# Attention of the second sequence: float32 in chunks of 64 steps in place of pairs of float16 parts

## The chip, the cores and the metric

One core of one Trainium2 chip runs the whole program. The metric is the device time of one launch in microseconds (us), lower is better, as the median of repeated runs. Engines: TensorE (PE, its weight loads shown apart as PEld), VectorE (DVE), ScalarE (ACT), GpSimd (POOL), and SyncE (SP), which here issues nearly all DMAs.

## What is computed

Four sequences of 768 steps with 8 heads of 48 pass through a decaying linear attention, and its output goes through two gated feed-forward layers; the second normalises its input first.

```python
# attention, per sequence and head (D = 48)
for t in range(S):
    cur = outer(u * k[t], v[t])
    y[t] = r[t] @ (state + cur)
    state = w[:, None] * state + outer(k[t], v[t])
# layer 1:  x = (silu(x @ Wg) * (x @ Wv)) @ Wo            (384 -> 1536 -> 384)
# layer 2:  the same on x / rms(x) * rms_g, with its own weights
```

Attention data are float32, the weights are doubles, read as pairs of 32-bit words and decoded on the chip.

## The kernel before, in words

The feed-forward layers run in blocks of 384 tokens, eight per layer (half a sequence each). Every float32 product is made of float16 products: each operand is held as a high and a low part, and three matmuls (high·high, high·low, low·high) take the place of one. A block is 12 steps; a step is the gate product `pg`, the value product `pv` (line 820) and the output product `po` (line 830), 27 matmuls of 384 columns. Between them ACT makes the silu (934), DVE the product `sl` (942, 944), ACT its high part (948) and POOL its low part (952). Blocks run in the order (layer 1, 0), (1, 1), (1, 2), (2, 0), (1, 3), (2, 1), ...

The weights are decoded by ACT and DVE, layer 1 as 12 large pieces, layer 2 as 36 of a third of that size (lines 769 to 810). Both layers stay on the core afterwards.

Attention comes in 32 units: 4 sequences, 2 halves of 384 steps, 4 pairs of heads. A unit has four matmul stages: `a` (keys by receptances inside a chunk, to PSUM `pa`), `d` (what each chunk adds to the state, `pd`), the state recurrence on DVE (`st`, line 654), and `y` (values by the masked `a`, and the state by receptances, `py`). The first sequence (units 0 to 7, class `Unit`) does this in float32 in chunks of 128 steps. The other 24 units (`SplitUnit`) do it in chunks of 64 steps in float16 pairs: four operands, the keys `k`, the receptances `r`, the weighted keys `e` and the masked product `a`, are split by ACT (line 566) and by POOL or DVE (line 569); the values are split and put into their columns of a zeroed tile `vb` by ACT and DVE (600, 602), the states into `sb` (665, 667). Each chunk of `a` and `d` is then three float16 matmuls for each head (line 622), each chunk of `y` six of 64 columns (line 611). ACT also sums the squares of `k`, `r` and `v` (line 607) for a range check at the end.

The order of every engine's instructions is fixed when the program is built. A planner (`Plan`, lines 71 to 135) gets each job with its engine, an assumed cost and the jobs it must follow, simulates the engines and always takes the ready job with the longest chain behind it. SP's DMA issues are ordered in the same way, as "D" jobs, and stand in one queue. A unit's jobs are named `lk`, `lr`, `nk`, `nr`, `nv` (loads), `tk`, `tr`, `kg`, `rg` (transposes and weighting), `k0` to `a1` (splits), `v0`, `v1`, `s0`, `s1` (values, states), `d`, `a`, `y`, `below`, `st`, `xh`, `xl` (lines 1103 to 1142).

Of the kernel before, what the change touches and what calls it, by code (L numbers as in the profile page):

```python
# [7 lines left out]
F32 = mybir.dt.float32  # L8
# [62 lines left out]
class Plan:  # L71
# [67 lines left out]
def fast_path(ctx, tc, r, k, v, w, u, wg1, wv1, wo1, wg2, wv2, wo2, rms_g, out):  # L139
# [11 lines left out]
    NG = TB // P  # L151
    NV = 4
    N2 = TB // C2
    NU1 = 2 * HP

    const = ctx.enter_context(tc.tile_pool(name="const", bufs=1))
    wp = ctx.enter_context(tc.tile_pool(name="wp", bufs=1))
# [38 lines left out]
    wsum = c_tile([P, 2 * NW], "wsum")  # L196
    mlo = c_tile([P, 1], "mlo")

    sqs = c_tile([P, 3 * (NBLK * HP - NU1)], "sqs")

# [130 lines left out]
    class Unit:  # L331
# [195 lines left out]
    class SplitUnit(Unit):  # L527


        def stage(self, slot):  # L530
            pass

        def load(self, which):
            t = b_tile([P, NP2 * D], "rts" if which else "kts", bufs=2)
# [43 lines left out]
            nc.vector.tensor_reduce(out=self.gd, in_=self.rk, axis=AX.X, op=ALU.add)  # L578

        def diagonals(self):  # L580
            self.af = b_tile([P, N2, C2], "af")
            nc.gpsimd.tensor_mul(self.af, late["id2"].unsqueeze(1).to_broadcast([P, N2, C2]),
                                 self.gd.unsqueeze(2).to_broadcast([P, N2, C2]))

        def decayed(self):
            self.ef = b_tile([P, N2, 64], "ef")
            kv = self.nk
            nc.gpsimd.tensor_mul(
                self.ef.rearrange("p c (i n) -> p c i n", i=2),
                bass.AP(kv.tensor, kv.offset, [list(kv.ap[0]), [D, N2], [16, 2], [1, 32]]),  # L590
                late["D2"][:, self.hp].rearrange("p (i n) -> p i n", i=2).unsqueeze(1).to_broadcast([P, N2, 2, 32]),
            )
# [10 lines left out]

        def squares(self, i):
            jk = ev.tile([P, N2, D], BF16, tag="sq", name="jk")
            col = 3 * (self.n - NU1) + i
            nc.scalar.activation(out=jk, in_=(self.nk, self.nr, self.nv)[i], func=AF.Square, accum_out=sqs[:, col : col + 1])

        def passes(self, out, pairs):
# [67 lines left out]

        yscale = 2.0 ** (X1S - 3 * AB)

    units = [(SplitUnit if b else Unit)(b, half, hp, (b * 2 + half) * HP + hp)  # L680
             for b in range(B) for half in range(2) for hp in range(HP)]

    bctx = ExitStack()
# [1 line left out]
    def open_split():  # L685
        actx.close()
        late["bp"] = bctx.enter_context(tc.tile_pool(name="bp", bufs=1))
        late["stg"] = bctx.enter_context(tc.tile_pool(name="stg2", bufs=1))
        for name in ("vb", "sb"):
            late[name] = b_tile([P, 2, N2, P], name, F16)  # L690
        late["G2"], late["F2"] = b_tile([P, HP, 2 * C2], "G2"), b_tile([P, HP, C2], "F2")
        late["D2"], late["u2"] = b_tile([P, HP, 64], "D2"), b_tile([P, HP, D], "u2")
        late["id2"], late["m2"] = b_tile([P, C2], "id2"), b_tile([P, C2], "m2", I32)
        late["carry"] = [b_tile([P, D], f"carry2{hp}") for hp in range(HP)]
        for j in range(2):
            nc.sync.dma_start(out=late["u2"][64 * j : 64 * j + 64], in_=bass.AP(u.tensor, D * j, [[0, 64], [2 * D, HP], [1, D]]))

    def split_zeros(name):
        nc.gpsimd.memset(late[name], 0.0)

    def split_tables():

# [256 lines left out]
    def check_range():  # L959


        n = 2 * NBLK * NG
        ns = 3 * (NBLK * HP - NU1)
        ok = ev.tile([P, n + n // 2 + 3 * NW + ns + 1], F32, tag="sq", name="ok")
        g2 = ev.tile([P, KT], F32, tag="g2", name="g2")
        gs = ev.tile([P, 1], F32, tag="gs", name="gs")
        nc.vector.tensor_mul(g2, rmsg, rmsg)
        nc.vector.tensor_reduce(out=gs, in_=g2, axis=AX.X, op=ALU.add)
        at = 0
        for i, bound, op in ((ssall, 3.0e38, ALU.is_le), (ssall[:, : n // 2], TOK_LO * DM, ALU.is_ge),  # L970
                             (wsum[:, :NW], SUM_HI, ALU.is_le), (wsum[:, :NF], MAG_MEAN * 3 * DM, ALU.is_ge),
                             (wsum[:, NF:NW], MAG_MEAN * DM, ALU.is_ge), (wsum[:, NW:], 0.0, ALU.is_le),
                             (sqs, MS_LO * N2 * D, ALU.is_ge), (gs, GAIN_LO, ALU.is_ge)):
            m = i.shape[1]
            nc.vector.tensor_scalar(out=ok[:, at : at + m], in0=i, scalar1=bound, scalar2=None, op0=op)
# [42 lines left out]
    def last(what, J):  # L1018
        return [(what, at_step[J] + NF - 1)] if J in at_step else []
# [30 lines left out]
    for un in units[:NU1]:  # L1050
# [23 lines left out]
        else:  # L1074
# [19 lines left out]
        add(("xl", n), "V", 0.47 * m, [("xh", n)], lambda un=un, j=j: un.x_lo(x_tile(j)),  # L1094
            soon=due(j, i))
    add("split", "D", 1.25, [("xl", n) for n in range(NU1)] + [("lo", 0, f) for f in range(NF)], open_split)
    for name in ("vb", "sb"):
        add(("z", name), "G", 1.32, ["split"], lambda name=name: split_zeros(name))
    add("tables2", "V", 2.2, ["split"], split_tables)
    add("dec2", "T", 0.5, ["tables2"], split_decay)  # L1100
    add("decay2", "A", 0.6, ["dec2"], split_decay2)
    add("u2", "G", 0.8, ["split"], split_bonus)
    for un in units[NU1:]:
# [8 lines left out]
        job_("lr", "D", 1.8, [("lk", n)] + p("tr", 2), lambda un=un: un.load(1))  # L1112
        for w_, users in (("k", ("rk", "ex", "sq")), ("r", ("rk", "sq")), ("v", ("v1", "sq"))):
            job_("n" + w_, "D", 0.9, [("lk", n)] + [x for us in users for x in p(us, 2)], lambda un=un, w_=w_: un.load_natural(w_))
        job_("tk", "V", 0.85, [("lk", n)] + p("k1"), lambda un=un: un.turn("k"))
# [9 lines left out]
        job_("eg", "G", 0.8, [("sums", n), "tables2"] + p("a1"), lambda un=un: un.diagonals())  # L1125
        job_("ex", "G", 1.0, [("nk", n), "decay2"] + p("e1"), lambda un=un: un.decayed())
        job_("e0", "A", 0.42, [("ex", n)] + p("d"), lambda un=un: un.split("e", 0))
        job_("e1", "G", 0.88, [("e0", n)], lambda un=un: un.split("e", 1, nc.gpsimd))
        job_("v0", "A", 0.8, [("nv", n), ("z", "vb")] + p("y"), lambda un=un: un.values(0))
# [7 lines left out]
        job_("st", "V", 1.5, [("d", n)] + p("s1") + ([("st", n - HP)] if un.half else p("st")), lambda un=un: un.states())  # L1137
        job_("s0", "A", 0.85, [("st", n), ("z", "sb")] + p("y"), lambda un=un: un.states2(0))
# [4 lines left out]
    add("attended", "D", 0.0, [("xl", n) for n in range(NU)] + [("sq", n) for n in range(NU1, NU)], close_attention)  # L1143


    def w_jobs(q, scale, wcost, ready, ahead):
# [252 lines left out]
```

## Time and profile before

| what | value |
|---|---|
| median of 3 runs | 1048.23 us (1045.59 to 1048.25) |
| the profiled execution: its own time | 1051.98 us |
| its span | 1050.3 us |
| PE busy | 978.8 us (93%) |
| PE weight load | 604.7 us (58%) |
| DVE busy | 609.4 us (58%) |
| ACT busy | 518.7 us (49%) |
| POOL busy | 456.9 us (43%) |
| mean granted PE clock | 0.968 |

Busy shares are averages over the whole span and hide that the engines' loads change along it. The page gives the span in 40 slices of 26 us with the busy tenths of each engine, and a view of chosen stretches gives the exact microseconds. The span ends with PE's work; the profiled execution's own time is 1.7 us longer than its span.

### The profile page before, as it was taken

What the parts mean: (1) busy time and instruction counts of PE and PEld (TensorE: products, weight loads), DVE (VectorE), ACT (ScalarE), POOL (GpSimd) and SP (SyncE); (2) the same over time, 40 slices, a digit from 0 to 9 for tenths busy, and PEclk for the clock granted to TensorE, in tenths of its full rate; (3) what the DMA queues carried; (4) which work ended last, traced back from release to release, by engine and by line L of the source; (5) the groups of instructions that cost most, each with busy time, mean ns of one, the idle gap of its engine ahead of it and who ended that gap; (6) DMA issues with size and microseconds to landing.
All of it is one profiled execution on the core that took longest, in us unless ns stands there. A gap on an engine that the chain in (4) does not pass through costs nothing.

```text
span 1050.3 us, 20693 instructions
## 1 busy us (share of the span) xinstructions
PE 978.8 (93%) x8061; PEld 604.7 (58%) x8062; DVE 609.4 (58%) x1120; ACT 518.7 (49%) x1217; POOL 456.9 (43%) x502
## 2 busy tenths in 40 slices
PE   7778798897889999999999999999999999999995
PEld 4645554554555566656666666666666666666663
DVE  6999999999888754546354744645352412231111
ACT  1965566767685743536344643455343523242322
POOL 6257376545455444553355444553444223332221
PEclk8898899998999999999999999999999999999998
DMA  7997155449655421213113321222010100200000
GB/s 181 222 224 190 27 132 150 113 74 183 142 161 70 103 71 27 49 40 92 40 41 63 80 53 37 30 61 69 7 18 8 54 1 1 53 23 1 23 1 27
DMA packets 152699, 77.13 MB, mean 73 GB/s; under 512 B 115472, under 2 KB 141200, under 8 KB 152592
## 3 DMA queue, kind: packets, MB, share of 16 engines
q1 hardware_dynamic: 152208, 75.13, 31.6%
q8 instruction: 65, 1.06, 0.5%
q0 software_dynamic: 384, 0.59, 0.3%
q14 instruction: 42, 0.34, 0.1%
HBM read 66.23 MB, written 9.45 MB: 72 GB/s over the span
## 4 chain that ended last, share of the span: by engine, by line
PE 65%; DVE 13%; DMA 11%; SPq 5%; issue 3%; ACT 2%; POOL 1%; DVEq 0%; ACTq 0%; POOLq 0%
PE pg L820 20%; PE pv L820 20%; PE po L830 20%; DMA raw<-in_moe_w_out_dram 5%; DMA raw<-in_moe_w_gate_dram 3%; DVE fi L787 2%; PE py L611 2%; DVE w L810 2%; SPq L364 2%; DVE fi L789 1%; DMA xs_d<-tt 1%; DVE fi L785 1%; PE pa L622 1%; PE pd L622 1%; DVE st L654 1%
## 5 line engine op out<-in xcount | busy, mean ns | idle before, releaser
L820 PEld LDWEIGHTS <-w 128*128 128x128 f16 x3456 | 337.8, 99 | 246.8 <-issue 35.6
L952 POOL TENSOR_TENSOR hl<-sl,hh 128x384 f16<-128x384 f32 x192 | 186.3, 971 | 432.8 <-ACT hh L948 402.4
L830 PE MATMUL po<-w,hh 128*128 128x384 f16 x1152 | 281.7, 327 | 0.5 <-DVE xo L844 0.5
L948 ACT ACTIVATE hh<-sl 128x384 f16<-128x384 f32 x192 | 100.0, 521 | 342.3 <-DVE sl L942 193.9
L830 PE MATMUL po<-w,hl 128*128 128x384 f16 x576 | 187.9, 326 | 7.2 <-POOL hl L952 7.2
L820 PE MATMUL pg<-xh,w 128*128 128x384 f16 x576 | 164.2, 341 | 15.1 <-DVE sl L944 14.6
L820 PE MATMUL pv<-x2v,w 128*128 128x384 f16 x864 | 157.6, 328 | 2.5 <-ACT sl L934 2.5
L942 DVE SCALAR_TENSOR_TENSOR sl<-sl,pv 128x384 f32<-128x384 f32 x96 | 52.9, 551 | 183.6 <-PE pv L820 175.0
L820 PE MATMUL pv<-xh,w 128*128 128x384 f16 x576 | 158.2, 330 | 0.0
L820 PE MATMUL pg<-x2g,w 128*128 128x384 f16 x864 | 156.1, 326 | 2.1 <-DVE sl L942 1.7
L830 PEld LDWEIGHTS <-hh 128*128 128x128 f16 x1152 | 111.8, 98 | 74.0 <-issue 1.5
L944 DVE TENSOR_TENSOR sl<-sl,pv 128x384 f32<-128x384 f32 x96 | 52.4, 547 | 102.3 <-PE pv L820 102.1
L934 ACT ACTIVATE sl<-pg 128x384 f32<-128x384 f32 x192 | 92.8, 484 | 32.7 <-PE pg L820 30.4
L820 PE MATMUL pg<-xl,w 128*128 128x384 f16 x288 | 98.4, 342 | 0.0
L820 PE MATMUL pv<-xl,w 128*128 128x384 f16 x288 | 95.1, 330 | 0.0
L830 PEld LDWEIGHTS <-hl 128*128 128x128 f16 x576 | 56.4, 98 | 47.8 <-POOL hl L952 11.0
L787 DVE SCALAR_TENSOR_TENSOR fi<-raw,fi 128x384 int32<-128x384 int32 (+1 forms) x48 | 43.6, 915 | 1.1
L810 DVE SCALAR_TENSOR_TENSOR w<-fi,w 128x384 f16<-128x384 f32 (+1 forms) x48 | 42.6, 902 | 0.8 <-ACT w L806 0.6
L654 DVE SCALAR_TENSOR_TENSOR st<-st,p,pd 128x48 f32<-128x48 f32 x120 | 31.8, 265 | 19.3 <-PE pd L622 15.1
L789 DVE SCALAR_TENSOR_TENSOR fi<-raw,fi 128x384 int32<-128x384 int32 (+1 forms) x48 | 40.0, 848 | 0.7
L569 POOL TENSOR_TENSOR ap<-af,ap 128x384 f16<-128x384 f32 x24 | 25.1, 1044 | 33.9 <-ACT ap L566 33.9
L551 DVE STREAM_TRANSPOSE kf<-kts 128x384 f32<-128x384 f32 x24 | 20.8, 865 | 32.4 <-POOL kp L569 32.3
(190 smaller groups left out, 1257.0 us busy)
## 6 DMA issues: line engine op xcount, KB each, us to landing
raw<-in_moe_w_out_dram SPq DMA_DIRECT2D x24, 384.0 KB, 4.4
kts<-in_k_dram SPq DMA_DIRECT2D x112, 70.0 KB, 2.5
rts<-in_r_dram SPq DMA_DIRECT2D x112, 70.0 KB, 2.1
raw<-in_moe_w_gate_dram SPq DMA_DIRECT2D x12, 384.0 KB, 3.9
raw<-in_moe_w_val_dram SPq DMA_DIRECT2D x12, 384.0 KB
xs_d<-tt SPq DMA_DIRECT2D x32, 144.0 KB, 2.9
xt<-xs_d SPq DMA_DIRECT2D x32, 144.0 KB, 3.0
out_dram<-xo SPq DMA_DIRECT2D x7, 576.0 KB, 3.1
```

The costliest lines, as they stand in the source:

```text
L569: eng.tensor_sub(t[:, 1], x, t[:, 0])
L654: nc.vector.scalar_tensor_tensor(out=st[:, c + 1], in0=st[:, c], scalar=self.w64(), in1=self.pd[:, c], op0=ALU.mult, op1=ALU.add)
L787: vec.scalar_tensor_tensor(out=fis[q], in0=high, scalar=-0x40000000, in1=fis[q], op0=ALU.bitwise_and, op1=ALU.bitwise_or)
L789: vec.scalar_tensor_tensor(out=fis[q], in0=low, scalar=29, in1=fis[q], op0=ALU.logical_shift_right, op1=ALU.bitwise_or)
L810: nc.vector.scalar_tensor_tensor(out=lo, in0=fis.pop(q).bitcast(F32), scalar=2.0**WS, in1=hi, op0=ALU.mult, op1=ALU.subtract)
L820: nc.tensor.matmul(pt, a[:, kt, :], x[:, kt, :], start=i == 0, stop=i == last)
L830: nc.tensor.matmul(po[g], a[:, sl], x, start=f == 0 and i == 0, stop=f == NF - 1 and i == 2)
L934: nc.scalar.activation(out=sl, in_=job[t]["g"], func=AF.Silu, scale=2.0 ** -(WS + (X2S if J[0] else X1S)))
L942: nc.vector.scalar_tensor_tensor(out=sl, in0=sl, scalar=2.0 ** (H2S - WS - V2S), in1=job[t]["v"], op0=ALU.mult, op1=ALU.mult)
L944: nc.vector.tensor_mul(sl, sl, job[t]["v"])
L948: nc.scalar.activation(out=job[t]["h"][0], in_=job[t]["sl"], func=AF.Copy)
L952: nc.gpsimd.tensor_sub(hl, job[t]["sl"], hh)
```

## The change

Units 8 to 15 (the second sequence) become a third class, `FullUnit`: float32 like the first sequence, but with the chunks of 64 steps and the loads of `SplitUnit`. It has no splits, no copies of the values, no low part of the states and no sums of squares. The values are loaded by DMA straight into their columns of a zeroed float32 tile: even units use the bytes of `vb`, odd units two half tiles with the tag `nv`. The even units' `kf`, `af` and `ef` use the tags of `SplitUnit`, the odd units' the bytes that later hold the float16 pairs. Units 16 to 31 stay as they were; their first units wait for the last `FullUnit` in some places, and `vb` and `sb` are zeroed again after it.

```diff
-    NU1 = 2 * HP
+    NU1, NU2 = 2 * HP, 4 * HP
+    class FullUnit(SplitUnit):
+        def slot(self, which):
+            return (which + "f", which + "p")[self.par]
+        def load_v(self):
+            for j in range(2):
+                for c, m, t in late["vf"][self.par]:
+                    nc.sync.dma_start(
+                        out=t[64 * j : 64 * j + 64, :, D * j : D * j + D],
+                        in_=bass.AP(v.tensor, self.off(j) + c * C2 * D, [[D, C2], [C2 * D, m], [1, D]]))
...
+        def mm_a(self):
+            self.pa = ps.tile([P, TB], F32, tag=self.bank(1), name="pa")
+            for c in range(N2):
+                for j in range(2):
+                    q = slice(64 * j, 64 * j + 64)
+                    nc.tensor.matmul(self.pa[q, C2 * c : C2 * c + C2], self.kf[q, c], self.rf[q, c], start=True, stop=True)
+        def mm_d(self):
...
+                    nc.tensor.matmul(self.pd[q, c], self.ef[q, c], self.values_of(c)[q, D * j : D * j + D], start=True, stop=True)
+        def states2(self):
+            c = 1 - self.half
+            for j in range(2):
+                q = slice(64 * j, 64 * j + 64)
+                nc.scalar.activation(out=late["sf"][q, c:, D * j : D * j + D], in_=self.st[q, c:N2], func=AF.Copy,
+                                     scale=self.w64()[q])
+        def mm_y(self):
...
+                mms = [(self.values_of(c), self.af[:, c])]
+                if self.half or c:
+                    mms.append((late["sf"][:, c], self.rf[:, c]))
+                self.passes(self.py[0 : 2 * D, C2 * c : C2 * c + C2], mms)
+    units = [(Unit, FullUnit, SplitUnit, SplitUnit)[b](b, half, hp, (b * 2 + half) * HP + hp)
+    for name in ("vb", "nv", "sb"):
+        add(("z", name), "G", 1.32, ["split"], lambda name=name: split_zeros(name))
     for name in ("vb", "sb"):
-        add(("z", name), "G", 1.32, ["split"], lambda name=name: split_zeros(name))
+        add(("z2", name), "G", 1.32, [("y", NU2 - 1)], lambda name=name: split_zeros(name))
+    for un in units[NU1:NU2]:
...
+        job_("nv", "D", 0.9, [("lk", n), ("z", ("vb", "nv")[un.par])] + p("y", 2), lambda un=un: un.load_v())
+        job_("tk", "V", 0.85, [("lk", n)] + p("a", 2), lambda un=un: un.turn("k"))
+        job_("kg", "V", 0.55, [("tk", n), "tables2"], lambda un=un: un.weigh("k"))
+        job_("tr", "V", 0.85, [("lr", n)] + p("y", 2), lambda un=un: un.turn("r"))
+        job_("rk", "G", 1.9, [("nk", n), ("nr", n), "u2"] + p("sums"), lambda un=un: un.products())
+        job_("eg", "G", 0.92, [("sums", n), "tables2"] + p("y", 2), lambda un=un: un.diagonals())
+        job_("ex", "G", 1.06, [("nk", n), "decay2"] + p("d", 2), lambda un=un: un.decayed())
+        job_("d", "T", 0.8, [("ex", n), ("nv", n), "decay2"] + p("below") + p("y"), lambda un=un: un.mm_d())
+        job_("a", "T", 0.9, [("kg", n), ("rg", n), ("d", n)] + p("xl"), lambda un=un: un.mm_a())
+        job_("below", "V", 0.55, [("a", n), ("eg", n)], lambda un=un: un.below())
+        job_("st", "V", 1.7, [("d", n)] + p("s0") + ([("st", n - HP)] if un.half else p("st")), lambda un=un: un.states())
+        job_("s0", "A", 0.9, [("st", n), ("z", "sb")] + p("y"), lambda un=un: un.states2())
+        job_("y", "T", 2.0, [("below", n), ("s0", n), ("a", n)], lambda un=un: un.mm_y())
...
+    for un in units[NU2:]:
...
+            job_("n" + w_, "D", 0.9, [("lk", n)] + [x for us in users for x in p(us, 2)] + ([("y", NU2 - 1)] if w_ == "v" and n < NU2 + 2 else []),
+        job_("tk", "V", 0.85, [("lk", n)] + p("k1") + q_("a"), lambda un=un: un.turn("k"))
+        job_("v0", "A", 0.8, [("nv", n), ("z2", "vb")] + p("y"), lambda un=un: un.values(0))
```

## Rows read from the trace of the kernel before

**Rows 1.** The page: busy time, and tenths in 40 slices of the span.
```profile
PE 978.8 (93%) x8061; PEld 604.7 (58%) x8062; DVE 609.4 (58%) x1120; ACT 518.7 (49%) x1217; POOL 456.9 (43%) x502
PE   7778798897889999999999999999999999999995
...
DVE  6999999999888754546354744645352412231111
...
PEclk8898899998999999999999999999999999999998
```

**Rows 2.** Stretches: length, busy PE PEld DVE ACT POOL, clock, DMA share, GB/s.
```profile
125.00:350.00 225.00, 194.51 (x1790) 117.45 (x1788) 209.56 (x390) 156.06 (x419) 119.39 (x128) 0.95 0.59 128
...
350.00:1050.00 700.00, 687.28 (x5657) 422.14 (x5654) 288.71 (x561) 290.44 (x668) 267.73 (x301) 0.99 0.17 38
...
275.00:300.00 25.00, 21.38 (x208) 12.89 (x207) 21.41 (x43) 19.65 (x54) 10.31 (x11) 0.93 0.61 165
...
325.00:350.00 25.00, 25.00 (x242) 15.58 (x241) 19.34 (x41) 14.65 (x41) 10.28 (x10) 1.00 0.67 95
```

**Rows 3.** PE's waits from 125 to 350 us: us in total, times, longest.
```profile
PE pg L820 <- DVE sl L944: 7.6, 5, 3.2
PE py L611 <- DVE sb L667: 7.5, 4, 4.1
PE py L611 <- POOL ap L569: 4.7, 5, 1.4
PE pv L820 <- ACT sl L934: 2.5, 1, 2.5
PE po L830 <- POOL hl L952: 2.4, 3, 1.5
PE py L611 <- ACT ap L566: 2.3, 2, 1.3
```

**Rows 4.** Groups of instructions by shape, 125 to 350 us: busy us, mean ns.
```profile
L787 DVE SCALAR_TENSOR_TENSOR fi<-raw,fi 128x384 int32<-128x384 int32 x36 | 24.1, 676 | 1.0
...
L569 DVE TENSOR_TENSOR rp<-rf,rp 128x384 f16<-128x384 f32 x9 | 10.6, 1180 | 0.7 <-ACT rp L566 0.7
...
L602 DVE SCALAR_TENSOR_TENSOR vb<-nv,vb 64x288 f16<-64x288 f32 x16 | 10.5, 654 | 0.2
...
L569 POOL TENSOR_TENSOR kp<-kf,kp 128x384 f16<-128x384 f32 x8 | 9.0, 1119 | 2.5 <-ACT kp L566 2.5
...
L667 DVE SCALAR_TENSOR_TENSOR sb<-st,p,sb 64x240 f16<-64x240 f32 x8 | 6.9, 856 | 0.1
...
L667 DVE SCALAR_TENSOR_TENSOR sb<-st,p,sb 64x288 f16<-64x288 f32 x6 | 3.8, 636 | 0.0
```

**Rows 5.** PE's timeline, float16 units: start, us, instructions.
```profile
165.05 0.75 PE L622 MATMUL pa<-rp,kp 64*64 64x64 f16 x36
...
202.24 0.75 PE L622 MATMUL pd<-vb,ep 64*64 64x48 f16 x36
```

**Rows 6.** Line 611 alone (float16 y), a stretch with one unit.
```profile
325.00:350.00 25.00, 1.21 (x36) 1.19 (x36) 1.00 0.67 95
```

**Rows 7.** PE's timeline, float32 units of the first sequence.
```profile
26.79 0.56 PE L470 MATMUL po<-vb,kg 128*64 128x48 f32 x12 [0.25 <-ACT kg L444]
...
29.49 0.73 PE L440 MATMUL in<-uw,kr 128*128 128x2 f32 x6
...
96.29 1.23 PE L463 MATMUL att<-rt,kt 64*128 64x128 f32 x12 [0.25 <-DVE kt L391]
```

**Rows 8.** Line 507 alone (float32 y, chunks of 128), a stretch with one unit.
```profile
75.00:100.00 25.00, 2.20 (x18) 2.26 (x18) 0.93 0.76 185
```

**Rows 9.** SP's timeline: issuing the values of one unit.
```profile
200.15 1.27 SPq L546 DMA_DIRECT2D nv<-in_v_dram  x2
```

**Rows 10.** DMA issues from 125 to 350 us: count, size, median us to landing.
```profile
nv<-in_v_dram SPq DMA_DIRECT2D x20, 72.0 KB, 2.7
```

**Rows 11.** Line 787 from 125 to 350 us: duration ns min/median/max.
```profile
L787 DVE SCALAR_TENSOR_TENSOR fi<-raw,fi x36: 527/559/1297, 145.4 to 345.6; 128x384 int32<-128x384 int32 x36
```

More of the change, by code (lines that the diff above doesn't have):

```diff
@@ L197, in fast_path @@
     mlo = c_tile([P, 1], "mlo")
-    sqs = c_tile([P, 3 * (NBLK * HP - NU1)], "sqs")
+    sqs = c_tile([P, 3 * (NBLK * HP - NU2)], "sqs")
     wu_raw = a_tile([2 * HP, 4, 32], "wu_raw")
@@ L527, in fast_path @@
     class SplitUnit(Unit):
-        def stage(self, slot):
-            pass
+        def slot(self, which):
+            return which + "f"
         def load(self, which):
@@ L580, in diagonals @@
         def diagonals(self):
-            self.af = b_tile([P, N2, C2], "af")
+            self.af = b_tile([P, N2, C2], self.slot("a"))
             nc.gpsimd.tensor_mul(self.af, late["id2"].unsqueeze(1).to_broadcast([P, N2, C2]),
@@ L585, in decayed @@
         def decayed(self):
-            self.ef = b_tile([P, N2, 64], "ef")
+            self.ef = b_tile([P, N2, 64], self.slot("e"))
             kv = self.nk
@@ L605, in squares @@
             jk = ev.tile([P, N2, D], BF16, tag="sq", name="jk")
-            col = 3 * (self.n - NU1) + i
+            col = 3 * (self.n - NU2) + i
             nc.scalar.activation(out=jk, in_=(self.nk, self.nr, self.nv)[i], func=AF.Square, accum_out=sqs[:, col : col + 1])
@@ L678, in fast_path, with slot, values_of, turn @@
         yscale = 2.0 ** (X1S - 3 * AB)
-    units = [(SplitUnit if b else Unit)(b, half, hp, (b * 2 + half) * HP + hp)
+    class FullUnit(SplitUnit):
+        def slot(self, which):
+            return (which + "f", which + "p")[self.par]
[5 more added lines that the diff above has]
+                        in_=bass.AP(v.tensor, self.off(j) + c * C2 * D, [[D, C2], [C2 * D, m], [1, D]]))
+        def values_of(self, c):
+            return next(t[:, c - c0] for c0, m, t in late["vf"][self.par] if c0 <= c < c0 + m)
+        def turn(self, which):
+            tag = "rp" if which == "r" else self.slot("k")
+            t = b_tile([P, N2, C2], tag, bufs=2 if which == "r" else 1)
+            setattr(self, which + "f", t)
+            nc.vector.transpose(
+                out=t.rearrange("q c t -> q (c t)").rearrange("q (p i) -> q i p", i=NP2),
+                in_=(self.kts if which == "k" else self.rts).rearrange("q (i d) -> q i d", d=D)[:, :, 0:32],
+            )
+        def mm_a(self):
[5 more added lines that the diff above has]
+        def mm_d(self):
+            self.nd = N2 - self.half
+            self.pd = ps.tile([P, N2, D], F32, tag=self.bank(0), name="pd")
+            for c in range(self.nd):
+                for j in range(2):
[3 more added lines that the diff above has]
+            c = 1 - self.half
+            for j in range(2):
+                q = slice(64 * j, 64 * j + 64)
+                nc.scalar.activation(out=late["sf"][q, c:, D * j : D * j + D], in_=self.st[q, c:N2], func=AF.Copy,
+                                     scale=self.w64()[q])
+        def mm_y(self):
+            self.py = ps.tile([P, TB], F32, tag=self.bank(2), name="py")
+            for c in range(N2):
+                mms = [(self.values_of(c), self.af[:, c])]
+                if self.half or c:
+                    mms.append((late["sf"][:, c], self.rf[:, c]))
+                self.passes(self.py[0 : 2 * D, C2 * c : C2 * c + C2], mms)
+        yscale = 2.0 ** (X1S - 2 * AB)
@@ L690, in open_split @@
             late[name] = b_tile([P, 2, N2, P], name, F16)
+        vf, late["sf"] = (late[name].bitcast(F32).rearrange("p a c m -> p (a c m)")[:, 0 : N2 * 2 * D].rearrange(
+            "p (c m) -> p c m", m=2 * D) for name in ("vb", "sb"))
+        late["vf"] = [[(0, N2, vf)], [(i * N2 // 2, N2 // 2, b_tile([P, N2 // 2, 2 * D], "nv", bufs=2)) for i in range(2)]]
         late["G2"], late["F2"] = b_tile([P, HP, 2 * C2], "G2"), b_tile([P, HP, C2], "F2")
@@ L698, in split_zeros @@
     def split_zeros(name):
-        nc.gpsimd.memset(late[name], 0.0)
+        for t in [t for _, _, t in late["vf"][1]] if name == "nv" else [late[name]]:
+            nc.gpsimd.memset(t, 0.0)
     def split_tables():
@@ L962, in check_range @@
         n = 2 * NBLK * NG
-        ns = 3 * (NBLK * HP - NU1)
+        ns = 3 * (NBLK * HP - NU2)
         ok = ev.tile([P, n + n // 2 + 3 * NW + ns + 1], F32, tag="sq", name="ok")
@@ L1102, in fast_path @@
     add("u2", "G", 0.8, ["split"], split_bonus)
-    for un in units[NU1:]:
+    for un in units[NU1:NU2]:
         n, hp, j, i = un.n, un.hp, un.n // HP, un.n % HP
@@ L1112, in fast_path @@
         job_("lr", "D", 1.8, [("lk", n)] + p("tr", 2), lambda un=un: un.load(1))
+        for w_, users in (("k", ("rk", "ex")), ("r", ("rk",))):
+            job_("n" + w_, "D", 0.9, [("lk", n)] + [x for us in users for x in p(us, 2)], lambda un=un, w_=w_: un.load_natural(w_))
+        job_("nv", "D", 0.9, [("lk", n), ("z", ("vb", "nv")[un.par])] + p("y", 2), lambda un=un: un.load_v())
+        job_("tk", "V", 0.85, [("lk", n)] + p("a", 2), lambda un=un: un.turn("k"))
+        job_("kg", "V", 0.55, [("tk", n), "tables2"], lambda un=un: un.weigh("k"))
@@ new lines, in fast_path, with job_ @@
+        job_("y", "T", 2.0, [("below", n), ("s0", n), ("a", n)], lambda un=un: un.mm_y())
+        job_("xh", "A", 0.47 * m, [("y", n)] + last("gv", (0, j - 2)), lambda un=un, j=j: un.x_hi(x_tile(j)))
+        job_("xl", "V", 0.55 * m, [("xh", n)], lambda un=un, j=j: un.x_lo(x_tile(j)), soon=due(j, i))
+    for un in units[NU2:]:
+        n, hp, j, i = un.n, un.hp, un.n // HP, un.n % HP
+        p = lambda what, back=1: [(what, n - back)] if (what, n - back) in plan.jobs else []
+        q_ = lambda what: [(what, n - 2)] if n == NU2 else []
+        m = len(un.rows())
+        def job_(name, eng, cost, after, fn, **kw):
+            add((name, n), eng, cost, after, fn, **kw)
+        job_("lk", "D", 1.8, ["split"] + p("tk", 2) + p("lr"), lambda un=un: un.load(0))
+        job_("lr", "D", 1.8, [("lk", n)] + p("tr", 2), lambda un=un: un.load(1))
@@ L1113, in fast_path @@
         for w_, users in (("k", ("rk", "ex", "sq")), ("r", ("rk", "sq")), ("v", ("v1", "sq"))):
-            job_("n" + w_, "D", 0.9, [("lk", n)] + [x for us in users for x in p(us, 2)], lambda un=un, w_=w_: un.load_natural(w_))
-        job_("tk", "V", 0.85, [("lk", n)] + p("k1"), lambda un=un: un.turn("k"))
+            job_("n" + w_, "D", 0.9, [("lk", n)] + [x for us in users for x in p(us, 2)] + ([("y", NU2 - 1)] if w_ == "v" and n < NU2 + 2 else []),
+                 lambda un=un, w_=w_: un.load_natural(w_))
@@ L1124, in fast_path @@
         job_("sums", "V", 0.37, [("rk", n)] + p("eg"), lambda un=un: un.sums())
-        job_("eg", "G", 0.8, [("sums", n), "tables2"] + p("a1"), lambda un=un: un.diagonals())
-        job_("ex", "G", 1.0, [("nk", n), "decay2"] + p("e1"), lambda un=un: un.decayed())
+        job_("eg", "G", 0.92, [("sums", n), "tables2"] + p("a1") + q_("y"), lambda un=un: un.diagonals())
+        job_("ex", "G", 1.06, [("nk", n), "decay2"] + p("e1") + q_("d"), lambda un=un: un.decayed())
         job_("e0", "A", 0.42, [("ex", n)] + p("d"), lambda un=un: un.split("e", 0))
         job_("e1", "G", 0.88, [("e0", n)], lambda un=un: un.split("e", 1, nc.gpsimd))
-        job_("v0", "A", 0.8, [("nv", n), ("z", "vb")] + p("y"), lambda un=un: un.values(0))
+        job_("v0", "A", 0.8, [("nv", n), ("z2", "vb")] + p("y"), lambda un=un: un.values(0))
         job_("v1", "V", 0.8, [("v0", n)], lambda un=un: un.values(1))
@@ L1136, in fast_path @@
         job_("a1", "G", 0.88, [("a0", n)], lambda un=un: un.split("a", 1, nc.gpsimd))
-        job_("st", "V", 1.5, [("d", n)] + p("s1") + ([("st", n - HP)] if un.half else p("st")), lambda un=un: un.states())
-        job_("s0", "A", 0.85, [("st", n), ("z", "sb")] + p("y"), lambda un=un: un.states2(0))
+        job_("st", "V", 1.5, [("d", n)] + p("s1" if n > NU2 else "s0") + ([("st", n - HP)] if un.half else p("st")), lambda un=un: un.states())
+        job_("s0", "A", 0.85, [("st", n), ("z2", "sb")] + p("y"), lambda un=un: un.states2(0))
         job_("s1", "V", 0.8, [("s0", n)], lambda un=un: un.states2(1))
@@ L1142, in fast_path @@
         job_("xl", "V", 0.47 * m, [("xh", n)], lambda un=un, j=j: un.x_lo(x_tile(j)), soon=due(j, i))
-    add("attended", "D", 0.0, [("xl", n) for n in range(NU)] + [("sq", n) for n in range(NU1, NU)], close_attention)
+    add("attended", "D", 0.0, [("xl", n) for n in range(NU)] + [("sq", n) for n in range(NU2, NU)], close_attention)
     def w_jobs(q, scale, wcost, ready, ahead):
```

2 lines of the change are left out of this document (added).

## The prediction, made before the changed kernel was run

> **What bounds the kernel now.** I read the page's slices first. PE stays at nine tenths or more only from the thirteenth slice on; before that it is mostly at seven or eight, and there DVE is at nine and eight, and hardly anywhere later [rows 1]. So there are two regimes. After 350 us PE is the bound: busy 687 of 700 us, DVE 41% [rows 2]. From 125 to 350 us, where the layer-2 weights are decoded, DVE is busy 209.6 of 225 us (93%) while PE is busy 194.5 (86%) and idle 30.5 [rows 2]. The second sequence's attention lies in this stretch: its values are split by line 602, 16 times, two for each of its eight units, all inside it [rows 4]. Since PE carries on without a gap afterwards, the time is PE's work plus PE's idle time, and an edit here counts by what it does to both.
>
> What PE waits for, from the view of waits: 27.0 of the 30.5 us stand in six rows [rows 3]. The `y` products wait 7.5 us for the low part of the states (DVE, 667), 4.7 for the low part of the masked product (POOL, 569) and 2.3 for its high part (ACT, 566): 14.5 us, each time for a link of the splitting that the change removes. The other 12.5 us are the feed-forward steps waiting for DVE's `sl`, ACT's silu and POOL's `hl`, which are late because they stand in queues behind other work. The granted clock is 0.95 in the mean there, so some 0.05 x 225 = 11 us of full-speed time are lost too; it is 0.93 in a stretch where PE idles 3.6 of 25 us and 1.00 where it idles for none [rows 2].
>
> **The change, part by part.**
>
> *DVE loses work.* `r1` goes: 10.6 us in nine, so 9.4 for eight units. `v1` goes: 10.5 us. `s1` goes: 6.9 + 3.8 = 10.7 us for the seven units that have it inside the stretch [rows 4]. Sum 30.6 us, and DVE's load falls from 209.6 to 179 us.
>
> *POOL and ACT lose work.* POOL loses three splits of a unit, each near the 9.0 us of `kp` in eight [rows 4], about 27 of its 119 us [rows 2]. ACT loses four splits, the values' copies and the squares. Neither is near full now; what this buys is shorter queues before `hl` and the silu, and I put that into the idle time below, not into a term of its own. Added on POOL are four memsets: two more before unit 8, beside the tables and the first loads, and two behind the `y` of unit 15, for which unit 16 waits. Unit 16 feeds block (1, 4), the seventh in order, whereas at 350 us the fourth, (2, 0), is being worked on; PE has other work, and DVE then has room. I cost them at nothing; without that cover it is a few us, once.
>
> *PE gets other matmuls.* A float16 unit costs 0.75 (`d`) + 0.75 (`a`) [rows 5] + 1.21 (`y`) [rows 6] = 2.7 us. In float32 each matmul becomes two instructions in the trace: `a` for one unit of the first sequence is 12 of 128 columns and 1.23 us, `d` is 12 of 48 columns and 0.56 [rows 7], `y` is 18 of 128 columns and 2.20 [rows 8]. With chunks of 64:
> - `a`: 24 of 64 columns, the same column count, at most 1.23 us. The two heads alternate between different rows and columns of the array. 36 such float16 matmuls take 0.75 us in `a`, but 36 of the same 64 columns take 1.21 in `y` [rows 5, 6], a ratio of 0.62, so the alternation pays: 0.76 at that ratio, half (0.62) at best. I take 0.85.
> - `d`: 24 of 48 columns, at most 2 x 0.56 = 1.12, at the ratio 0.69, at best 0.56. I take 0.75.
> - `y`: 24 of 64 columns, each with a fresh weight load of 96 float32 columns. By columns alone 2.20 / 18 / 2 x 24 = 1.47 us. But six loads of 128 float32 columns with hardly a matmul behind them took 0.73 us [rows 7], 0.12 each, so 0.09 for 96 columns, which 64 columns don't cover: 24 x 0.09 = 2.2. I take 2.1, nearer to the loads.
>
> Sum 3.7, that is +1.0 us a unit and **+8 us** in all; the ends are 2.65 (nothing added) and 4.55 (+15 us). This is wholly on the path.
>
> *The chain of a unit gets shorter.* `y` follows `below` and `s0` at once. The 14.5 us of waits of `y` lose their releasers. Late next are the high part of the states on ACT and `below` on DVE, both already done when PE resumed in those waits; but DVE's queue still lies before them, so I leave 3 us. The remaining 16 us (12.5 named, 3.5 in small pieces) hang on queues that get shorter, DVE's by 15% and POOL's by 23%; I leave 12. So 15 of 30.5 us stay and **15.5 us** come back. Another way to the same number: idle by DVE's share. At 86% (21.41 of 25 us) PE idled 3.6 us, at 77% for none [rows 2]; 179 us in some 215 is 83%, between them 2.4 us in 25, or 20 us left and 10 back. I take the first, as the waits that go are named one by one, and keep the second for the range.
>
> *Clock.* Of the 11 us I take **3** back, as the gaps shrink; the ends are none and 6.
>
> *Loads.* Odd units load their values with four DMAs instead of two: two issues took 1.27 us [rows 9], so 5 us more on SP over four units, in a queue that is not full. The new wait is that the values go straight into the tile that the `y` two units earlier reads, so their load stands in SP's queue until then, with the next unit's loads and a weight piece behind it. The `a` of unit 9 is at 165 us and the `d` of unit 11 at 202 [rows 5]; landing takes 2.7 us [rows 10]. With `y` of unit 9 some ten us behind its `a`, over 20 us are left. Nothing.
>
> **Sum.** +8 - 15.5 - 3 = -10.5 us. The profiled execution took 1051.98 us (1.7 more than its span), so 1041.5; that execution is 3.75 above the median of the runs, 1048.23, and from there it is **1038 us**.
>
> **A rule weighed.** The mean of line 787 is 676 ns, its least 527 [rows 11], so DVE's operations in this stretch are stretched by something: 36 x 0.15 = 5.4 us for this line. The Trainium skill ("SBUF — State Buffer", Who interferes with whom) says that a DVE instruction with two SBUF inputs and a GpSimd instruction that reads SBUF exclude each other. By that rule the 23% less POOL work would give DVE back another 1.2 us on this line and, as an estimate, 5 us on all lines like it, of which some 3 would reach the time: 1035 instead of 1038. The spread of the row fits it but does not name POOL as the cause.
>
> **The rivals.**
> 1. *DVE was the whole bound.* All its 30.6 us count: PE's idle time falls to 5 us and 6 us of clock return. 8 - 25.5 - 6 = -23.5: 1025 us. For it: DVE at 93%. Against: PE alone would need 194.5 + 8 - 6 = 196.5 us of a stretch then 201.5 long, 97.5%, with DVE at 89%, while it idled 14% at DVE's 86% [rows 2]. Chance 0.15.
> 2. *It cancels.* The idle time by DVE's share is right (10 back) and the clock gives nothing: +8 - 10 = -2, 1046 us. Chance 0.17.
> 3. *Slower: the waits are handed on.* PE's order is fixed, and with the shorter chain the planner puts each `y` earlier, so that PE meets DVE's queue before `st` and `below` instead of the splits behind them. Only 5 us come back, while float32 costs between my value and the upper end, 11.4: +6.4, 1054.6 us. It decides from the point where less than PE's added work comes back. For it: the two longest waits in the first two rows are for DVE [rows 3]. Against: 7.0 us of the `y` waits were for POOL and ACT. Chance 0.13.
>
> My forecast has 0.55. Its own range is 1033 to 1044. The range to hold 8 in 10 takes rivals 1 and 2 in and reaches into 3: 1026 to 1050. A measurement can tell about 0.3% (3.1 us) from no change: faster 0.70 (forecast, rival 1), same 0.17 (rival 2), slower 0.13 (rival 3).
>
> **What would show it.** From 125 us to PE's saturation: PE's share at or above 91% and DVE's at or below 87%; `y` (24 instructions) near 2.1 us, `a` 0.85, `d` 0.75; no more than 3 us of waits of `y`; saturation some ten us earlier than 325. It is wrong if `y` still waits over 8 us (rival 3), if DVE stays above 90% with PE idle for 20 us or more (rival 2), or if float32 costs over 4.2 us a unit.

## The result: 1% faster

The changed kernel takes 1038.75 us (median of 6 runs, 1035.55 to 1042.67) against 1048.51 (6 runs of the kernel before, beside it); the ratio is 0.9902, 95% interval 0.9877 to 0.9928. The prediction was 1038. Measured once more, beside the last experiments, the ratio was 0.9908 (0.9883 to 0.9933). The profiled execution took 1040.54 us, its span is 1038.5.

The page after: the busy line, and PE, DVE and PE's clock in 40 slices, which answer to [rows 1].

```profile
PE 982.7 (95%) x7786; PEld 613.8 (59%) x7786; DVE 573.1 (55%) x1080; ACT 486.6 (47%) x1121; POOL 442.5 (43%) x482
...
PE   6787898989999999999999999999999999999996
...
DVE  6899997988787544655354645555342412241111
...
PEclk7889899999999999999999999999999999999998
```

The span is 11.8 us shorter, while PE is busy 3.9 us longer (982.7 against 978.8): so its idle time fell by 15.7 us, from 71.5 to 55.8. DVE lost 36 us of work, ACT 32, POOL only 14.

The same stretches as in [rows 2] (length, busy PE, PEld, DVE, ACT, POOL, clock), and the first one in two parts:

```profile
125.00:350.00 225.00, 209.13 (x1621) 132.67 (x1620) 186.99 (x367) 129.15 (x327) 108.09 (x114) 0.98 0.57 130
...
125.00:225.00 100.00, 90.96 (x732) 58.50 (x731) 90.01 (x177) 54.24 (x134) 52.68 (x54) 0.97 0.58 136
225.00:350.00 125.00, 118.17 (x891) 74.17 (x890) 96.97 (x191) 74.91 (x194) 55.40 (x60) 0.99 0.55 125
```

and the two parts in the kernel before:

```profile
125.00:225.00 100.00, 85.93 (x855) 52.38 (x853) 97.92 (x183) 72.49 (x193) 57.38 (x61) 0.97 0.51 124
225.00:350.00 125.00, 108.58 (x937) 65.07 (x936) 111.64 (x208) 83.56 (x226) 62.01 (x68) 0.93 0.66 132
```

In the stretch PE's idle time went from 30.5 to 15.9 us and the clock from 0.95 to 0.98, and DVE from 93% to 83%. In its first part DVE had been at 98%, in the second at 89%; PE's idle time fell by 5.0 us in the first part and by 9.6 in the second, so most of it came back behind the part where DVE was fullest. The rest of PE's idle time, outside the stretch, is nearly as it was.

PE's waits from 125 to 350 us after (us in total, times, longest), which answer to [rows 3]:

```profile
PE po L894 <- POOL hl L1016: 8.7, 4, 4.5
PE py L612 <- DVE ap L639: 3.1, 2, 1.7
PE pg L884 <- DVE sl L1008: 2.6, 2, 2.5
PE py L612 <- DVE af L639: 1.4, 2, 1.0
```

The waits of `y` fell from 14.5 to 4.5 us, and what is left of them is for `below` (line 639 now). Of the feed-forward waits, those for the silu are gone and those for `sl` fell from 7.6 to 2.6 us (line 944 before, 1008 now), while those for `hl` grew from 2.4 to 8.7. (`ap` and `af` here are both the float32 masked product, of odd and even units.)

What a float32 unit costs PE: the timeline of `d` and `a` in one unit, and line 612 alone in a stretch with one unit's `y`.

```profile
146.36 0.90 PE L720 MATMUL pd<-vb,ef 64*64 64x48 f32 x24
...
148.76 0.92 PE L712 MATMUL pa<-rp,kf 64*64 64x64 f32 x24
```

```profile
300.00:325.00 25.00, 2.17 (x24) 2.20 (x24) 1.00 0.48 103
```

0.90 + 0.92 + 2.17 = 4.0 us against 2.7 [rows 5, 6]. In the timeline of `y` each pair of matmuls starts 0.17 us after the last, 85 ns for one. The second pair of numbers in the row above is PEld's: the 24 weight loads are busy 2.20 us, as long as the matmuls.

### The profile page after: what moved, and what is told of

Read it like the earlier page. It is cut to its first block, busy times and chain, and to the rows that moved or that the text cites. A ratio compares the mean times of both kernels' runs of the same rounds, so it can differ in the third digit from the quotient of the medians.

```text
span 1038.5 us, 19984 instructions
## 1 busy us (share of the span) xinstructions
PE 982.7 (95%) x7786; PEld 613.8 (59%) x7786; DVE 573.1 (55%) x1080; ACT 486.6 (47%) x1121; POOL 442.5 (43%) x482
## 4 chain that ended last, share of the span: by engine, by line
PE 75%; DVE 10%; DMA 7%; SPq 3%; issue 2%; ACT 1%; POOL 1%; DVEq 0%; ACTq 0%; POOLq 0%
PE pg L884 24%; PE po L894 23%; PE pv L884 23%; DMA raw<-in_moe_w_out_dram 3%; PE py L612 2%; DMA raw<-in_moe_w_val_dram 2%; DVE fi L851 2%; DVE fi L853 2%; SPq L365 1%; PE pa L623 1%; PE pd L623 1%; DVE w L874 1%; DMA first<-in_r_dram 1%; DVE fi L849 1%; DVE st L655 1%
## 5 line engine op out<-in xcount | busy, mean ns | idle before, releaser
L884 PE MATMUL pg<-xh,w 128*128 128x384 f16 x576 | 161.2, 336 | 10.8 <-DVE sl L1008 10.8
L853 DVE SCALAR_TENSOR_TENSOR fi<-raw,fi 128x384 int32<-128x384 int32 (+1 forms) x48 | 43.1, 912 | 0.7
L851 DVE SCALAR_TENSOR_TENSOR fi<-raw,fi 128x384 int32<-128x384 int32 (+1 forms) x48 | 42.7, 894 | 1.2
L833 ACT ACTIVATE mag<-raw 128x384 bf16<-128x384 f32 (+1 forms) x48 | 35.1, 732 | 12.9 <-DMA raw<-in_moe_w_out_dram 4.4
L874 DVE SCALAR_TENSOR_TENSOR w<-fi,w 128x384 f16<-128x384 f32 (+1 forms) x48 | 40.5, 863 | 0.0
L870 ACT ACTIVATE w<-fi 128x384 f16<-128x384 f32 (+1 forms) x48 | 32.0, 677 | 14.1 <-DVE fi L853 13.9
```

What stands on the lines that cost most here:

```text
L833: nc.scalar.activation(out=mags[q], in_=word_views(raws[q])[1].bitcast(F32), func=AF.Abs, accum_out=wsum[:, w_col(q) : w_col(q) + 1])
L851: vec.scalar_tensor_tensor(out=fis[q], in0=high, scalar=-0x40000000, in1=fis[q], op0=ALU.bitwise_and, op1=ALU.bitwise_or)
L853: vec.scalar_tensor_tensor(out=fis[q], in0=low, scalar=29, in1=fis[q], op0=ALU.logical_shift_right, op1=ALU.bitwise_or)
L874: nc.vector.scalar_tensor_tensor(out=lo, in0=fis.pop(q).bitcast(F32), scalar=2.0**WS, in1=hi, op0=ALU.mult, op1=ALU.subtract)
L884: nc.tensor.matmul(pt, a[:, kt, :], x[:, kt, :], start=i == 0, stop=i == last)
```

## The experiments

All ratios are to the kernel before, run beside them; the changed kernel's 0.990 is the mark. 0.001 is 1 us. For several runs PE's idle time from 125 to 350 us is given too. It is 30.5 us before, 15.9 in the changed kernel and 18.8 in a second profile of the changed kernel (last section), so differences of some 3 us in it lie within what two executions of one program show.

**DVE's work back, beside the chain.** Changed kernel, with three jobs more for each float32 unit:

```diff
+        job_("er", "V", 0.47, [("rg", n), ("z", "dj")], lambda un=un: un.extra_r())   # tensor_sub on rf, as r1
+        job_("ev", "V", 0.8, [("nk", n), ("z", "dj")], lambda un=un: un.extra_v())    # two of 64x288, as v1
+        job_("es", "V", 0.8, [("s0", n), ("z", "dj")], lambda un=un: un.extra_s())    # two on st, as s1
```

> The changed kernel with the DVE work of the three removed splits put back for units 8 to 15 (five instructions of the same shapes, on a scratch tile), but behind nothing that y, a or d of the same unit waits for. The chain of a unit stays short, DVE's load is back at what it was (about 30 us more in the stretch). My theory (part of the gain is the shorter chain of y, part the shorter queues): between the two kernels, 1043 to 1047 us, y still waiting under 6 us, and the waits for sl growing again. Rival D (DVE's load is the whole reason): the idle time comes back entire while PE still pays 8 us, 1050 to 1055. Rival C (the chain is the whole reason): no more than 3 us above the changed kernel, 1039 to 1042.

Measured: 0.9992 (0.9972 to 1.0011). The whole net gain (what is left after PE's higher price) is lost, 9 us, give or take 3: between what my theory and rival D expected. PE idles 25.6 us in the stretch, so 9.7 of the 14.6 us are back. (Beside the chain means that nothing of the same unit waits for these jobs; the next unit's `st` waits for `es`, as it waited for `s1` in the kernel before.) PE's waits in the stretch, without two of 0.2 us:

```profile
PE po L913 <- POOL hl L1035: 10.1, 3, 6.1
PE pg L903 <- DVE sl L1027: 6.4, 3, 2.5
PE pv L903 <- ACT sl L1017: 4.6, 1, 4.6
PE py L612 <- DVE af L639: 2.7, 2, 2.4
PE py L612 <- DVE ap L639: 1.3, 2, 1.2
```

`y` waits as little as in the changed kernel (4.0 us), its chain is as short, and yet nothing is won in time: the feed-forward steps wait instead. DVE is back at 208.58 of 225 us:

```profile
125.00:350.00 225.00, 199.39 (x1533) 125.56 (x1530) 208.58 (x395) 123.52 (x314) 106.11 (x112) 0.95 0.57 126
```

So a short chain of `y` is not enough for the gain. Rival C is out.

**The links back, without DVE.** Changed kernel:

```diff
-        job_("y", "T", 2.0, [("below", n), ("s0", n), ("a", n)], lambda un=un: un.mm_y())
+        job_("s1c", "A", 0.9, [("s0", n)], ...   # ACT: sf = Copy(sf), two halves
+        job_("a0c", "A", 0.42, [("below", n)] + p("a1c"), ...  # ACT: copy of af
+        job_("a1c", "G", 0.95, [("a0c", n), ("z", "on")], ...  # POOL: af = copy * 1
+        job_("y", "T", 2.0, [("a1c", n), ("s1c", n), ("a", n)], lambda un=un: un.mm_y())
```

> The changed kernel with two links put back between below and y (a copy on ACT, a product with ones on POOL) and a second pass over the states on ACT between s0 and y, so that y stands behind as many links as before, without any work for DVE. POOL gets 1 us a unit more, ACT 1.6. My theory: the waits of y come back in part, 1043 to 1048 us. Rival C (the chain is the whole reason): 1048 to 1052. Rival D (DVE's load): 1039 to 1042.

Measured: 0.9923 (0.9892 to 0.9954), 2 us above the changed kernel's ratio, which its interval includes; by that interval it may be some 5. Four of the waits:

```profile
PE pg L899 <- DVE sl L1023: 6.4, 3, 3.5
PE po L909 <- POOL hl L1031: 6.3, 3, 2.7
PE py L612 <- POOL af L741: 4.3, 2, 2.5
PE py L612 <- POOL ap L741: 2.1, 2, 1.5
```

`y` does wait for the restored link, 6.4 us, but no longer for `below`, and the waits for `hl` are 6.3 us here, so that PE idles 18.5 us in the stretch. It is against rival C again, and nearest to rival D. The links stand on engines with room (ACT busy 136 of 225 us, POOL 112); a link in DVE's own queue, as `s1` was, was not put back.

**Both together.** Changed kernel with both edits.

> The changed kernel with both edits of the earlier runs together: the DVE work of three splits back beside the chain, and the links on ACT and POOL back between below, s0 and y. What is left of the change then is PE's float32, four of six splits less on POOL and ACT each, and the missing squares. If the sum of my terms holds, the gain is lost and most of PE's 8 us show: ratio to the kernel before 1.001 to 1.006. If the DVE load was all (with it back, y is late through DVE anyway and the links change nothing more): the same as with the DVE work alone, 0.997 to 1.001. If the links and the load are each enough to hold y up, but not added: also near that, with the waits of y named for POOL and ACT.

Measured: 0.9963 (0.9947 to 0.9979), and 22.0 us of idle time. The links add nothing to the DVE work, though `y` waits 6.7 us for POOL's link; if anything the two together are faster than the DVE work alone. That could be a different order by the planner, which was not tried. My terms do not add.

**The kernel before without the low parts on DVE.** Float16 kept; for units 8 to 15 `r1`, `v1` and `s1` are not made. The matmuls stay as many as they were, some of them with a high part in place of the missing low one, so the result of these units is wrong; only the time is of use.

```diff
-            for i, (m, n) in enumerate(((0, 0), (0, 1), (1, 0))):
+            for i, (m, n) in enumerate(((0, 0), (0, low), (1, 0))):     # low = 0 for b == 1
+        less = {"r1": "r0", "v1": "v0", "s1": "s0"}                      # for units below 16 the later job is not added
```

> The kernel before, float16 throughout, with the low parts of the receptances, the values and the states left out for units 8 to 15 (so their result is coarser): DVE loses the same 30 us as in the change, the number of matmuls stays (the high part is used twice), POOL and ACT keep their splits, and y still stands behind the masked product's two links. My theory: DVE's queue and the state link give back 11 to 15 us and nothing is paid on PE: 1033 to 1038 us. Rival D: 1028 to 1033, all of the idle time of the stretch but a few us. Rival C: only the 7.5 us of the state link's waits, 1040 to 1043.

Measured: 0.9939 (0.9914 to 0.9965), 6 us faster than before: less than my theory or D expected, and inside what rival C gave. The stretch, four of PE's waits in it, then two of DVE's:

```profile
125.00:350.00 225.00, 191.59 (x1783) 116.37 (x1782) 190.77 (x352) 154.08 (x419) 121.58 (x130) 0.95 0.58 127
...
PE pg L820 <- DVE sl L944: 10.4, 4, 3.6
PE py L611 <- POOL ap L569: 8.5, 4, 4.9
PE pg L820 <- DVE sl L942: 7.8, 2, 7.6
PE py L611 <- ACT ap L566: 4.6, 2, 2.9
...
DVE fi L785 <- DMA raw<-in_moe_w_val_dram: 8.2, 2, 8.0
DVE fi L785 <- DMA raw<-in_moe_w_out_dram: 5.0, 4, 3.3
```

Here the waits were handed on, as my third rival had it: with the state link gone (7.5 us before), `y` waits 13.1 us for the masked product's two links instead of 7.0. And one weight piece, 15 us in landing, held the now faster DVE for 8 us, and PE behind it for 7.6; such a landing, 14.5 us, was there before too, and DVE waited for it less than 3 us. DVE is busy 85% of the stretch here, about as in the changed kernel (83%), and yet PE idles 33.4 us, more than before; without that one wait of 7.6 it would be 25.8 at best. So less work for DVE is not enough either. What is left here and gone in the changed kernel is the splitting on ACT (busy 154 us in the stretch, 129 in the changed kernel) and on POOL (122 and 108), with its links before `a`, `d` and `y`. Rival C's number is not its mechanism: the waits of `y` did not fall by the 7.5 us of the state link but by 1.4.

**POOL's work back, beside the chain.** Changed kernel, three jobs more for each float32 unit:

```diff
+        job_("gk", "G", 0.88, [("kg", n), ("z", "dj")], ...   # POOL: tensor_sub of kf, f16 out
+        job_("ge", "G", 0.88, [("ex", n), ("z", "dj")], ...   # the same of ef
+        job_("ga", "G", 0.88, [("below", n), ("z", "dj")], ...  # the same of af
```

> The changed kernel with three subtractions a unit put back on POOL (same shapes as the three removed splits, on a scratch tile), not on the chain of y: POOL's load in the stretch up by some 25 us. My theory puts little on POOL's relief (hl is a little earlier): 0 to 3 us above the changed kernel, ratio to before 0.990 to 0.993. Rival P (POOL's queue before hl, and its reads against DVE's, made up a good part of the gain): 5 to 9 us above, ratio 0.995 to 0.999, hl waits well above 8.7 us and DVE's decoding lines longer in the mean.

Measured: 0.9950 (0.9928 to 0.9972), 5 us above the changed kernel, give or take 3: rival P's lower end. But PE does not wait more for `hl`, as that rival had it; it waits more for `below`:

```profile
PE po L899 <- POOL hl L1021: 6.0, 3, 3.4
PE py L612 <- DVE ap L639: 5.1, 3, 3.5
PE pg L889 <- DVE sl L1013: 4.0, 3, 2.2
PE py L612 <- DVE af L639: 2.3, 2, 1.7
```

By the time POOL's relief counted, and I had put no term of its own on it. The profile does not show where the 5 us lie: PE idles 18.3 us in the stretch, inside the spread of the changed kernel. DVE's decoding is slower with it: the three lines of the decoding that read two tiles (shapes of 384) sum to 75.1 us here and to 71.0 and 68.5 in the two profiles of the changed kernel. The rows of the first are

```profile
L853 DVE SCALAR_TENSOR_TENSOR fi<-raw,fi 128x384 int32<-128x384 int32 x36 | 25.2, 714 | 0.7
L851 DVE SCALAR_TENSOR_TENSOR fi<-raw,fi 128x384 int32<-128x384 int32 x36 | 23.2, 650 | 1.1
...
L874 DVE SCALAR_TENSOR_TENSOR w<-fi,w 128x384 f16<-128x384 f32 x36 | 22.6, 652 | 0.0
```

**Float32 for the third sequence too.** `NU1, NU2 = 2 * HP, 6 * HP`.

> The changed kernel with the third sequence in float32 too, where PE had no idle time to give back. It measures the price of a float32 unit on PE by itself. My sum (+1.0 us a unit on PE, wholly on the path): 8 us above the changed kernel, 1045 to 1049 us. Rival (the price is hidden or much smaller than the rows of the first sequence say): no more than 3 us above it, 1038 to 1042.

Measured: 0.9988 (0.9967 to 1.0010), 9 us above the changed kernel, as the sum had it. PE's busy time says the same without a stopwatch:

```profile
PE 992.6 (94%) x7509; PEld 624.0 (59%) x7510; DVE 547.5 (52%) x1040; ACT 453.4 (43%) x1025; POOL 418.8 (40%) x458
```

992.6 - 982.7 = 9.9 us for eight units, 1.2 each. DVE lost 25.6 us of work, ACT 33.2 and POOL 23.7, and it bought nothing, since PE had no idle time there.

**Each `y` twice.** Changed kernel, `for _ in range(2)` around the passes of `y`, the planner's costs unaltered.

> The changed kernel with every y product done twice over (the second pass overwrites the first), with the same order of jobs. It asks how much of PE work added in this stretch reaches the time: 24 more float32 instructions a unit, 2.0 us, 16 us in all. If PE's work is wholly on the path, as my sum has it: 14 to 16 us above the changed kernel, ratio to before 1.003 to 1.006. If what idle time is left swallows some of it: 5 to 12 us above, ratio 0.995 to 1.002.

Measured: 0.9975 (0.9952 to 0.9997), 7 us above the changed kernel, give or take 3, for 15 us of matmuls (line 612 is busy 32.5 us in the stretch, 17.5 in the changed kernel). About half of it does not reach the time. The profile began at a clock of 0.92, as the second profile of the changed kernel did. Beside that one PE is busy 18.8 us longer over the span and idle 7.7 us less, and the span is 11.1 us longer. So PE's work is not "wholly on the path" there, as I had put it: part of it falls into time in which PE would have stood idle.

**The first half of the sequence only.** `NU2 = 3 * HP`, units 12 to 15 as `SplitUnit`. (The state that passes between the two forms is not rescaled, so those four units' result is off.)

> Float32 for units 8 to 11 only, units 12 to 15 in float16 pairs as before. My theory: the gain comes from the whole stretch in which DVE is full, so half the units give about half: ratio 0.993 to 0.997 (4 to 7 us above the changed kernel). Rival E (only the early units matter, where DVE is at 98%; the later four only pay for PE): the same as the changed kernel or a little faster, 0.986 to 0.991. Rival L (only the later ones, just before PE saturates): as the kernel before, 0.998 to 1.002.

Measured: 0.9909 (0.9887 to 0.9931): the same as with all eight units, so rival E. The later four units, in the part where DVE was at 89%, only repay PE's price. By the profiles: PE's idle time over the span is 71.5 us before, 61.9 here and 55.8 with all eight, while PE is busy 980.2 us here and 982.7 with all eight. So the first four units bring 9.6 us of idle time, and the second four another 6.1 for the price of four units, 5.0 us.

**Versions that follow from this.** If DVE's queue is the bound and ACT now has room, move work from DVE to ACT. First the normalisation between the layers:

```diff
-            nc.vector.tensor_scalar_mul(xo[:, g], xo[:, g], ri[:, 0, g : g + 1])
+            nc.scalar.activation(out=xo[:, g], in_=xo[:, g], func=AF.Copy, scale=ri[:, 0, g : g + 1])
...
-            add(("sc", blk), "V", 1.0, ...
+            add(("sc", blk), "A", 1.5, ...
```

> The changed kernel with the normalisation between the two layers (three multiplications by a column per block, 5.7 us of DVE in the stretch) moved from DVE to ACT, which the change left at 57%. If DVE's load is what counts in the stretch at the rate that its 31 us put back have shown (9 us of time for 31 of load): 1 to 2 us faster than the changed kernel, ratio to before 0.987 to 0.990. Rival (DVE is no longer the bound there): no difference.

then also the float32 units' diagonals from POOL (six copies of `id2`, each scaled by a column of `gd`):

> The same, and the diagonals of the float32 units (0.93 us of POOL each, 7.5 us in all) made by ACT as six small copies scaled by a column. POOL's 25 us put back cost 3 to 7 us of time, so 1 to 2 us more: ratio to before 0.985 to 0.989. Rival (ACT's queue before the silu and hh gets longer by what POOL's gets shorter): as without it, 0.987 to 0.991.

or, in place of that, a second of the three evacuations of each output block (`if g:` for `if g == 1:`):

> The normalisation and one more of the three evacuations of each block's output on ACT in place of DVE (1.6 us of DVE in the stretch, 8 over the whole span). By DVE's load in the stretch: 0.5 us faster than with the normalisation alone, ratio 0.986 to 0.990. Rival (the end of the program waits for two evacuations in a row on ACT): 0.5 us slower than that.

with the changed kernel beside them:

> The changed kernel itself once more, unaltered, beside the three others, so that they are compared on one chip: ratio to the kernel before 0.988 to 0.993, as in its first measurement.

| kernel | median us | ratio to before (95%) |
|---|---|---|
| changed, again | 1041.26 | 0.9908 (0.9883 to 0.9933) |
| normalisation on ACT | 1034.95 | 0.9837 (0.9814 to 0.9861) |
| and diagonals on ACT | 1033.04 | 0.9830 (0.9805 to 0.9855) |
| normalisation and evacuation on ACT | 1032.18 | 0.9810 (0.9784 to 0.9835) |

The normalisation alone is worth 6 us, three times and more what its 5.7 us of DVE time promised by the rate of the first experiment; the other two moves add 1 and 2 to 3 us, inside each other's intervals. All three beat both kernels. The gain is made before layer 2 begins: the first layer-2 gate product starts at 283.7 us with the normalisation on ACT, 289.3 in the changed kernel (with a granted clock of 0.85 up to 125 us, as against 0.86), 295.5 before. Why it is so much was not tried. The first normalisation starts at 162.1 us on ACT and at 198.1 on DVE in the changed kernel, though DVE's waits in the stretch there do not name POOL's result `ri`, for which the normalisation stands.

```profile
L884 PE MATMUL pg<-x2g,w x864: 326/326/337, 289.3 to 1021.6; 128*128 128x384 f16 x173
```

```profile
L884 PE MATMUL pg<-x2g,w x864: 326/326/337, 283.7 to 1016.0; 128*128 128x384 f16 x173
```

(The first is the changed kernel, the second the one with the normalisation on ACT: durations, then first and last start.)

## Why the prediction was right, and where its reasons were not

- *Two regimes, and the time as PE's work plus PE's idle time.* Right: the same float32 gains where DVE is full (second sequence) and costs 9 us where PE is (third). Of the signs, PE's share (93%) and DVE's (83%) came, and PE's last wait in the stretch ends at 308 us instead of 321; the waits of `y` are 4.5 us where I wanted at most 3.
- *PE's price, +8 us.* 4.0 us a unit were measured where I had 3.7: `d` 0.90 for 0.75, `a` 0.92 for 0.85, `y` 2.17 for 2.1. So about +10 (9.9 by the third sequence's busy time). The reading of `y` as bound by its weight loads held (85 ns for 90, against 61 by columns alone); for `a` and `d` I counted on somewhat too much overlap of the two heads: 0.75 and 0.80 of the times of the first sequence (1.23 and 1.12), where I took 0.69 and 0.67.
- *Idle time, -15.5 us.* -14.6 in the stretch, -15.7 over the span. Right in size.
- *Clock, -3 us.* PE's busy time rose by 3.9 us where some 9.9 were added: 6 us came back, the upper end of my bounds. It is a remainder of the sum, put down to the clock, whose mean rose from 0.968 to 0.973. +10 - 15.7 - 6 = -12 for the span; the profiled executions differ by 11.4 us, the medians by 9.8.
- *Where the idle time comes from.* This step failed. I gave 11.5 of the 15.5 us to the links that go out of `y`'s chain. The links did go out and the waits of `y` fell to 4.5 us, but links put back on ACT and POOL cost 2 us, within error, while DVE work put back beside the chain cost the whole net gain with the chain still short, and brought 9.7 of 14.6 us of idle time back. The releaser named in a wait is only the last of those that are late, and PE, in fixed order, waits for the next one if that is taken away. DVE's load is not the whole cause either: with DVE at 85% in float16 PE idled 33.4 us, so the second of my two ways, by DVE's share alone, fails there. Before PE's price is paid the change brings some 20 us; put back one at a time, DVE's work costs 9 of them, POOL's 5 and the links 2, and they don't add. What makes up the rest stays open: ACT lost 32 us of work, and no run put that back alone.
- *POOL's relief.* I costed it at nothing of its own; putting its work back cost about 5 us. POOL's busy time fell by 14 us, not by 27: the splits that went had taken 26, but the four memsets added 3.4, and some of its remaining operations took longer.
- *PE's added work on the path.* Half of the doubled `y` did not show. The terms are not independent: what PE gets is partly taken from its own idle time. That the sum came out within 1 us is partly luck: the price was 2 us too low and the clock gave back 3 us more than I took, and the idle time came out right though it was put down to the wrong links.
- *The rule weighed.* By the Trainium skill's page "SBUF — State Buffer" (Who interferes with whom) less reading by POOL should have shortened DVE's decoding. From before to after it hardly did: the three lines sum to 71.5 us before and to 71.0 and 68.5 in the two profiles after. With POOL's work put back they rose to 75.1. The sign agrees with the rule, but the size is near the 2.5 us between two executions of one kernel, and the 5 us that I estimated for all lines of this kind did not come: of the 36 us that DVE lost over the span, 34 are the splits themselves (11.8 of `rp`, 10.5 of `vb`, 12.0 of `sb`).
- *Rivals.* "DVE was the whole bound" (1025 us) came too far but named the engine that counted most. "It cancels" (1046) did not come: 15.7 us of idle time came back, not 10. "The waits are handed on" did not decide here, but is what the float16 kernel with less DVE work showed.

## What to carry to other kernels

Before crediting a gain to a wait that an edit removes, look whether the engine that ended it is full over the stretch, and put work and links back one at a time. Here the work taken off the full engine counted for more (9 us) than the links themselves (2 us), but less work on that engine alone, with the float16 splits left on the other engines, brought only 6. A more expensive form on the matmul engine can pay in a stretch where another engine is at 98%, and costs its full price where the matmul engine is; so choose the form by stretch, not for the whole kernel. After such a change, try to move work from the still fuller engine to the one that it emptied: that was worth another 6 to 9 us here.

## What had not been expected of the hardware

The same changed kernel ran its first 125 us at a granted clock of 0.85 in one profile and 0.92 in another, with PE busy 95.31 and 92.72 us there; layer 2 then began at 289.3 and 281.1 us, and the spans were 1038.5 and 1032.3.

```profile
0.00:125.00 125.00, 95.31 (x595) 64.49 (x596) 107.04 (x168) 71.33 (x130) 70.63 (x74) 0.85 0.70 172
```

```profile
0.00:125.00 125.00, 92.72 (x638) 62.28 (x640) 111.72 (x175) 75.66 (x137) 70.87 (x75) 0.92 0.73 175
```

Its six first runs lie between 1035.55 us (clock 0.981 in the mean) and 1042.67 (0.970), the faster the higher the clock. In both profiles PE stands idle from about 10 to 15 us, and the clock falls to 0.50 (1.2 GHz) there; in the first it is back at 1.00 (2.4 GHz) from 35 us, in the second from 25. So how long PE runs at the lower level after the gaps of the start differs between executions of one program, and that would account for much of the spread of the runs; it was not traced for the others. A single profile can't tell 5 us here; the timed ratios can.
